# Later stores, first weights in two halves, and a refinement moved one stage on, in a fused state-space and feed-forward kernel

## The chip, the cores and the metric

The kernel runs on one core of a Trainium2 chip. The metric is the device time of one execution in microseconds; lower is better. A core has five engines that run their own instruction streams in order: TensorE (PE; its weight loads are shown as PEld), VectorE (DVE), ScalarE (ACT), GpSimdE (POOL) and SyncE (SP). DMA transfers are issued from the queues of SP, ACT and POOL.

## The reference

Two branches are computed from the layer-normalised input and added to the input itself. Sizes: L = 2048 positions, D = 576 channels, N = 128 states per channel, F = 4608 hidden units.

```
xn  = layernorm(x)                                   # per row of 576
dt  = exp(log_dt);  logdA = dt * (A_re + i A_im)
K[d, l] = Re sum_n C[d,n] * exp(logdA[d,n] * l) * dt[d] * B[d,n]     # l = 0..2047
y   = causal convolution over l of xn[:, d] with K[d, :]  (by FFT)  +  xn * Dskip
ffn = silu(xn @ w1) @ w2                              # (2048x576)(576x4608)(4608x576)
out = x + y + ffn
```

## The kernel before

**What is on TensorE.** Every float32 product is made from a high and a low part of each operand (three matmuls: high·high, high·low, low·high). ScalarE copies the high part (a cast), VectorE subtracts to get the low part. So each input block and each weight block needs a ScalarE copy and a VectorE subtraction before TensorE can use it: `put_xt` (L118) transposes a normalised block on TensorE into `pt`, makes `xh` (L123) and `xl` (L125); `split_w1` (L266) makes `w1h` (L274) and `w1l` (L276); `split_w2` (L286) does it for w2 (L292, L294); `up` (L298) makes the first product `ph` (L306 to L308), and from it `gf` (Silu, L314), `gh` (L315) and `gl` (L316); `down` (L318) makes the second product `po` (L336) and adds it to `acc` (L341).

**Stages.** The feed-forward part walks over two halves of the rows, nine chunks of hidden units and two blocks of 512 rows (the last chunks by a scheme of seven products for eight, `wino_ffn`). A second stream, `side()` (L1045), is woven into it step by step:

- `phase0` (L204): loads row blocks j in pairs, normalises them (`norm`, L179), turns them (`turned`, L222) and stores the normalised rows to the DRAM tensor `dxn` (L235), which only `spread` reads, much later. Blocks 8 to 15 also store their transposed form to `dxt` (L234) through one buffer `xt`, and are loaded back in the second half of the kernel.
- `natural` (L655): from A, B, C and log_dt the small tables f, rho, phi (128 states x 576 channels) and four real powers of the decay per channel, `ex`. It is a generator of several stages: after tanh (L705) comes a stage with the reciprocal root `r` (L709), its square (L710), three refinement operations on each of four column groups (L715 to L717), a store to `dexp` (L718) and the products of C and B up to L738; then a stage with Arctan (L742), a second reciprocal root (L744) and what follows.
- `kgen` (L772): 36 steps on VectorE and ScalarE that make tables S and C from f, rho, phi and pieces of `dexp` (`eb`, L802), multiplied on TensorE to `kp` (L883), `z` (L898), and stored to `d1k`. `spread` (L139) runs beside it.
- `spectral` (L919) and `tail` (L977): the convolution in the frequency domain and the way back.

**What sets the order.** The program is written in the order of the generators; a scheduler then places instructions on each engine's queue by its own estimate of times, so that neighbours can pass each other. Each engine executes its queue in order and waits on semaphores. `behind(ins)` keeps an instruction from being placed before `ins`. `tc.high_priority()` lets gf, gh, gl and the accumulations go ahead. `pins["gh"]` is the last `gh` written so far, `pins["sd"]` the last power of a variance on GpSimdE (L191).

**The first microseconds.** SP and ACT issue eight loads for row blocks 0 and 1, SP then six for the first two weight tiles `w1r` (`load_w1`, L245; each tile is 640 rows by 256 columns and is split in halves of 128), four for blocks 2 and 3, four for w2, eight for blocks 4 to 7. GpSimdE computes the powers of the variances and issues the `dxn` stores.

Of the kernel before, what the change touches and what calls it, by code (L numbers as in the profile page):

```python
# [10 lines left out]
F32 = mybir.dt.float32  # L11
F32R = mybir.dt.float32r
AF = mybir.ActivationFunctionType
ALU = mybir.AluOpType
# [3 lines left out]
P = 128  # L18
L = 2048
D = 576  # L20
# [21 lines left out]
def kernel(  # L42
# [21 lines left out]
    nc = tc.nc  # L64
# [18 lines left out]
    dxn = dram.tile([P, NJ, D], F32, name="dxn")  # L83
    dw2 = dram.tile([NFT - WINO_C * FT, P, 2, D], F32, name="dw2")
    dexp = dram.tile([P, 4 * D], F32, name="dexp")
# [26 lines left out]
    def new_xt(blk):  # L112
        xh = xtp.tile([P, NKT, 512], F32R, tag="xh", name=f"xh_{blk}")
        xl = xtp.tile([P, NKT, 512], F32R, tag="xl", name=f"xl_{blk}")
        x4 = xtp.tile([P, 512], F32R, tag="x4", name=f"x4_{blk}")
        return xh, xl, x4

    def put_xt(xh, xl, x4, src, low=None):  # L118

        pt = pss.tile([P, NKT, P], F32, tag="pss", name="pt")  # L120
        for kt in range(NKT):
            nc.tensor.transpose(pt[:, kt, :], src[:, kt * P:(kt + 1) * P], ident)
        nc.scalar.copy(xh, pt)  # L123
        with behind(low):
            nc.vector.tensor_sub(xl, pt, xh)  # L125
        pt = pss.tile([P, 512], F32, tag="pss", name="pt4")
        nc.tensor.transpose(pt[:64, :P], src[:, NKT * P:D], ident)
        pins["xt_s"] = nc.scalar.copy(x4[:64, :], pt[:64, :P]).ins
        pins["xt_v"] = nc.vector.tensor_sub(x4[64:, :], pt[:64, :P], x4[:64, :]).ins

    xts = {}
    pairs = {}
    pins = {}
    wino = {}

    def behind(ins):
        return tc.issue_after(ins) if ins is not None else nullcontext()
# [66 lines left out]
    def phase0(p0, js):  # L204
        j0 = js[0]
        if j0 < 8:
            xs = load_x(j0, accp, "acc", (nc.sync, nc.scalar) if j0 == 0 else (nc.sync,))
            acc.update(zip(js, xs))
            yield
        else:  # L210
            xs = load_x(j0, p0, "xj", (nc.sync,))
        if j0:
            with behind(pins["xt1"] if j0 == 2 else None):
                turned(p0, js, norm(p0, js, xs))
        else:
            xn = [norm(p0, (j,), (xj,)) for j, xj in zip(js, xs)]
            last = pins["xn"]
            for j in js:
                turned(p0, (j,), xn[j], None if j else last)
                pins[f"xt{j}s"] = pins["xt_s"]  # L220

    def turned(p0, js, xn, low=None):  # L222
        for i, j in enumerate(js):
            b, jj = divmod(j, 4)
            if b < 2:
                if jj == 0:
                    xts[b] = new_xt(b)
                c = slice(jj * P, (jj + 1) * P)
                xh, xl, x4 = xts[b]
                put_xt(xh[:, :, c], xl[:, :, c], x4[:, c], xn[:, i, :], low)  # L230
            else:
                xt = p0.tile([P, 9, P], F32R, tag="xt", name="xt", bufs=1)
                put_xt(xt[:, 0:4, :], xt[:, 4:8, :], xt[:, 8, :], xn[:, i, :])
                nc.gpsimd.dma_start(dxt[b - 2][:, :, jj * P:(jj + 1) * P], xt.bitcast(F32))  # L234
        nc.gpsimd.dma_start(dxn[:, js[0]:js[0] + len(js)], xn[:, :len(js)])  # L235

    def ffn():
        w2v = w2.rearrange("(t p) d -> p t d", p=P)
# [6 lines left out]
        def load_w1(half, c, t):  # L245

            f = c * FT + t
            first = half == 0 and c == 0
            r1 = (pa if first and t else w1x if t and w1x else wp).tile([P, 5, 2 * P], F32, tag="w1r", name="w1r", bufs=1)
            fs = slice(f * P, (f + 2) * P)  # L250
            eng = nc.sync
            eng.dma_start(r1[:, 0:4, :], w1[0:512, fs].rearrange("(k p) f -> p k f", p=P))
            eng.dma_start(r1[0:64, 4, :], w1[512:576, fs])
            pins["load"] = eng.dma_start(r1[64:128, 4, :], w1[512:576, fs]).ins
            R1[half, c, t] = r1

        def need_w1(half, c, t):
            if (half, c, t) not in R1:
                load_w1(half, c, t)

        def next_w1(half, c, t):
            new = (half, c + 1) if c + 1 < NCH else (half + 1, 0)
            if w1x and new < (1, WINO_C):
                load_w1(*new, t)
# [89 lines left out]
        for t in (0, 2):  # L354
            load_w1(0, 0, t)
# [17 lines left out]
        first, end = WINO_C * FT // 2, NFT // 2  # L373
# [39 lines left out]
        for i, blk in enumerate(plain[:-1]):  # L413
            half, c, b = blk
# [14 lines left out]
            for step in ("u0", "d0", "d1", "d2", "d3", "u1", "u2", "u3"):  # L429
                k = int(step[1])  # L430
# [224 lines left out]
    def natural(nat):  # L655
# [3 lines left out]
        v = nc.vector  # L659

        def tl(name):
            return nat.tile([NP, NT, NS], F32, tag=name, name=name)
# [34 lines left out]
        v.tensor_mul(aim, aim, dtb)  # L697
        lrT = nat.tile([P, D], F32, tag="lrT", name="lrT")
        turned(are, lrT)
        turned(aim, fT)  # L700

        ex = nat.tile([P, 4 * D], F32, tag="ex", name="ex")
        r = nat.tile([P, 4 * D], F32, tag="r", name="r")
# [3 lines left out]

        with behind(pins["gh"]):
            nc.scalar.activation(r, ex, AF.Abs_reciprocal_sqrt, bias=neg1)  # L709
        nc.scalar.activation(r, r, AF.Square)  # L710
        for i in range(0, 4 * D, D):

            c = slice(i, i + D)
            e = nat.tile([P, D], F32, tag="lrT", name="e")
            v.scalar_tensor_tensor(e, ex[:, c], 1.0, r[:, c], op0=ALU.subtract, op1=ALU.mult)  # L715
            v.scalar_tensor_tensor(r[:, c], e, 2.0, r[:, c], op0=ALU.add, op1=ALU.mult)
            v.scalar_tensor_tensor(ex[:, c], ex[:, c], 1.0, r[:, c], op0=ALU.add, op1=ALU.mult)  # L717
        nc.sync.dma_start(dexp, ex)  # L718
        pr, pi, t0, t1 = tl("pr"), tl("pi"), tl("t0"), tl("t1")
        v.tensor_mul(pr, cr, br)  # L720
        v.tensor_mul(t0, ci, bi)
# [16 lines left out]
        v.tensor_scalar(t1, t1, 1.0, None, op0=ALU.add)  # L738
        yield

        with behind(pins["gh"]), behind(pins["xo"]):
            last = nc.scalar.activation(t0, t0, AF.Arctan).ins  # L742
        with behind(last):
# [301 lines left out]
    def side():  # L1045
# [13 lines left out]
        with tc.tile_pool(name="kf", bufs=1) as kfp:  # L1059
            for n in ("f", "rho", "phi"):  # L1060
                kf[n] = kfp.tile([P, D], F32, name=n + "T")
            with tc.tile_pool(name="nat", bufs=1) as nat, tc.tile_pool(name="pb", bufs=2) as pb:
                nt = natural(nat)
                tiles = iter(range(8, NJ, 2))
                for at, tables in ((0.0, 1), (0.02, 0), (0.035, 0), (gate_of(1), 1), (0.06, 0), (gate_of(2), 1), (0.08, 0), (0.085, 1)):
                    yield at
                    if tables:
                        next(nt, None)
                    else:
                        j = next(tiles)  # L1070
                        with behind(pins["gl"]):
                            for _ in phase0(pb, (j, j + 1)):
                                pass
            with behind(pins["sd"]):
                nc.gpsimd.dma_start(f1, cf1)
            nc.sync.dma_start(vt, cv)
            with tc.tile_pool(name="up", bufs=1) as up, tc.tile_pool(name="w1x", bufs=1) as more:
                sp = spread(up)
                for n, at in enumerate(kgen()):
                    if n > 1:  # L1080
                        w1x = more
                        next(sp, None)
                    yield marks[0] + at * (marks[1] - marks[0])
                for _ in sp:
                    pass
# [16 lines left out]
    sd, fg = side(), ffn()  # L1102
# [85 lines left out]
```

## Time and profile before

| | |
|---|---|
| median of 3 runs | 1108.67 us (1108.48 to 1112.02) |
| profiled execution | 1109.05 us |
| its span, first to last instruction | 1107.2 us |
| granted TensorE clock, mean | 0.999 |
| busy, TensorE / VectorE / ScalarE / GpSimdE | 1089.8 / 949.5 / 722.3 / 141.1 us |
| moved by DMA | 173.67 MB |

The profile shows one execution. "Busy" counts the time in which an engine has at least one instruction running. In a timeline row the first number is the start in us, the second the duration; then engine, source line, operation, output tile <- input tiles, shapes, the number of merged instructions, and in brackets the idle time of that engine just before and what released it. A row of waits gives the total, the number of times and the longest.

### The profile page before, as it was taken

How to read it: one execution, taken by the hardware profiler on the slowest of the kernel's cores; microseconds unless marked ns; L12 is line 12 of the kernel's file. 1: busy time of each engine (PE TensorE's matmuls, PEld its weight loads, DVE VectorE, ACT ScalarE, POOL GpSimd, SP SyncE). 2: the span in 40 equal slices, each digit the busy share in tenths (PEclk: the TensorE clock that was granted, in tenths of full speed). 3: DMA queues.
4: the chain of work that ended last, by engine and by line, in shares of the span. 5: the costliest groups of instructions: out<-in, count | busy, mean ns of one | idle time of the engine just before them, and what ended most of it. 6: DMA issues, size and time to landing. Idle time of an engine off the chain costs nothing.

```text
span 1107.2 us, 23071 instructions
## 1 busy us (share of the span) xinstructions
PE 1089.8 (98%) x9101; PEld 986.7 (89%) x9101; DVE 949.5 (86%) x1615; ACT 722.3 (65%) x1284; POOL 141.1 (13%) x246
## 2 busy tenths in 40 slices
PE   6999999999999999999999999999999999999998
PEld 5988989898998888898999899899999999999787
DVE  6699989999999999999999997988988888886323
ACT  4475456676777676766767656877777787775320
POOL 1112100000000000000330002111111211111220
PEclk9999999999999999999999999999999999999999
DMA  8536552355253534447974246455555655554984
GB/s 255 162 109 217 167 166 89 115 145 153 94 161 110 144 132 119 166 110 260 236 197 93 81 88 193 146 173 177 150 163 177 181 167 155 178 161 107 242 222 112
DMA packets 162412, 173.67 MB, mean 157 GB/s; under 512 B 88560, under 2 KB 128128, under 8 KB 161664
## 3 DMA queue, kind: packets, MB, share of 16 engines
q1 hardware_dynamic: 137360, 105.35, 34.5%
q0 software_dynamic: 24272, 65.38, 19.4%
q10 hardware_dynamic: 672, 1.48, 0.5%
q8 instruction: 72, 1.18, 0.4%
q14 instruction: 36, 0.29, 0.1%
HBM read 109.64 MB, written 62.60 MB: 156 GB/s over the span
## 4 chain that ended last, share of the span: by engine, by line
PE 85%; DVE 5%; DMA 4%; ACT 3%; issue 1%; SPq 0%; POOL 0%; ACTq 0%; DVEq 0%
PE po L336 38%; PE ph L306 18%; PE pb L463 6%; PE pc L463 3%; PE kp L883 3%; PE pk L1017 2%; PE pu L1017 2%; PE pb L1017 2%; PE pa L463 2%; PE z L898 1%; PE ph L308 1%; PE ph L307 1%; DMA acc<-in_A_u_dram 1%; DMA kl<-d1k 1%; PE pc L469 1%; PE pu L155 1%
## 5 line engine op out<-in xcount | busy, mean ns | idle before, releaser
L336 PE MATMUL po<-w,gh 128*128 128x288 f32 x2304 | 474.2, 296 | 0.9 <-DVE acc L341 0.9
L336 PEld LDWEIGHTS po<-w,gh 128*128 128x128 f32 x2304 | 375.2, 188 | 16.7 <-issue 3.3
L336 PE MATMUL po<-w,gl 128*128 128x288 f32 x1152 | 333.6, 295 | 0.0
L336 PEld LDWEIGHTS po<-w,gl 128*128 128x128 f32 x1152 | 214.9, 188 | 1.7
L341 DVE TENSOR_TENSOR acc<-po,acc 128x288 f32<-128x288 f32 x296 | 129.7, 450 | 54.6 <-PE po L336 53.2
L306 PE MATMUL ph<-xh,w1h 128*128 128x512 f32 (+1 forms) x368 | 99.7, 388 | 1.7 <-ACT gf L314 1.3
L306 PE MATMUL ph<-xh,w1l 128*128 128x512 f32 (+1 forms) x368 | 98.3, 384 | 0.0
L306 PE MATMUL ph<-xl,w1h 128*128 128x512 f32 (+1 forms) x368 | 98.2, 384 | 0.0
L314 ACT ACTIVATE gf<-ph 128x512 f32<-128x512 f32 (+1 forms) x92 | 53.0, 578 | 51.4 <-PE ph L308 32.4
L306 PEld LDWEIGHTS ph<-xl,w1h 128*128 128x128 f32 x368 | 68.0, 191 | 13.4
L306 PEld LDWEIGHTS ph<-xh,w1l 128*128 128x128 f32 x368 | 66.7, 190 | 12.2 <-DVE w1l L276 0.2
L306 PEld LDWEIGHTS ph<-xh,w1h 128*128 128x128 f32 x368 | 65.0, 191 | 12.0 <-ACT gf L314 1.9
L840 ACT ACTIVATE c<-th,magic 128x1040 f32<-128x1040 f32 x36 | 42.0, 1167 | 41.5 <-DVE C L861 27.4
L158 POOL DMA_DIRECT2D d1u<-u x32 | 17.5, 547 | 393.9 <-ACT u L157 392.5
L842 ACT ACTIVATE c<-th 128x1040 f32<-128x1040 f32 x36 | 38.7, 1075 | 41.0 <-DVE th L841 41.0
L316 DVE TENSOR_TENSOR gl<-gf,gh 128x512 fp32r<-128x512 f32 (+1 forms) x92 | 60.2, 657 | 4.0 <-ACT gh L315 3.7
L922 POOL DMA_DIRECT2D m<-in_cm_dram x64 | 33.9, 531 | 215.8 <-PE pu L1017 135.9
L315 ACT CAST gh<-gf 128x512 fp32r<-128x512 f32 (+1 forms) x92 | 55.2, 603 | 8.9 <-PE po L336 7.9
L480 DVE TENSOR_TENSOR gl<-gf,gh 128x512 fp32r<-128x512 f32 x56 | 37.8, 688 | 23.1 <-ACT gh L479 22.7
L860 DVE TENSOR_TENSOR S<-th,C 128x1024 f32<-128x1024 f32 x36 | 43.9, 1218 | 7.4 <-ACT th L843 7.3
L841 DVE SCALAR_TENSOR_TENSOR th<-c,th 128x1040 f32<-128x1040 f32 x36 | 44.3, 1231 | 0.3 <-ACT c L840 0.3
L824 DVE TENSOR_TENSOR th<-vt,fT 128x1040 f32<-128x1040 f32 x36 | 44.2, 1231 | 0.2
(269 smaller groups left out, 2370.9 us busy)
## 6 DMA issues: line engine op xcount, KB each, us to landing
w1r<-in_B_w_dram SPq DMA_DIRECT2D x36, 512.0 KB, 4.1
dw<-w SPq DMA_DIRECT2D x28, 576.0 KB, 4.7
w<-dw POOLq DMA_DIRECT2D x28, 576.0 KB, 5.8
w2r<-in_B_w_dram SPq DMA_DIRECT2D x44, 288.0 KB, 4.7
d1u<-u POOLq DMA_DIRECT2D x32, 288.0 KB, 2.8
d1k<-stage SPq DMA_DIRECT2D x18, 512.0 KB, 6.4
ul<-d1u SPq DMA_DIRECT2D x32, 288.0 KB, 2.9
kl<-d1k SPq DMA_DIRECT2D x32, 288.0 KB, 3.6
```

The lines of the kernel that those rows point to most:

```text
L306: nc.tensor.matmul(ph, w[:, kt, :], v[:, kt, a:e], start=n + kt == 0, stop=False)
L314: nc.scalar.activation(gf, ph, AF.Silu)
L315: pins["gh"] = nc.scalar.copy(gh, gf).ins
L316: pins["gl"] = nc.vector.tensor_sub(gl, gf, gh).ins
L336: pins["pe"] = nc.tensor.matmul(po[:, :HD], gs[g][:, js], ws[:, w, hs], start=n == 0 and j not in begun, stop=n == 3 * len(terms) - 1, ski ...
L341: nc.vector.tensor_add(acc[j][:, hs], po[:, :HD], acc[j][:, hs])
L463: pins["pe"] = nc.tensor.matmul(dst, a[:, kt], v[:, kt], start=start and n == 0, stop=stop and n == 5, skip_group_check=True).ins
L824: nc.vector.tensor_mul(split(th), row(vt[:, 0:65], 65), col(fT, i, 65))
L840: nc.scalar.activation(c65, th, AF.Identity, bias=magic)
L841: nc.vector.scalar_tensor_tensor(th, c65, MAGIC, th, op0=ALU.subtract, op1=ALU.subtract)
L860: nc.vector.tensor_mul(ov3, t[:, :, 0:64].rearrange("n d (x y) -> n d x y", y=32), mv3)
L1017: nc.tensor.matmul(dst, st, mv[:, hs], start=n == 0, stop=n == 3 * len(terms) - 1)
```

## The change

Three edits:

1. `turned` no longer issues the store to `dxn` directly: it appends it to a list `held`, and from the second pair of blocks on all held stores are issued, each behind the last power of a variance. So the stores of blocks 0 and 1 come after the power for blocks 2 and 3, together with the store of that pair.
2. The first weight tile is loaded in two column halves of 128, the first from ScalarE's queue, the second from SP's; three DMAs become six.
3. In `natural` the square of `r`, the twelve refinement operations and the store to `dexp` leave the stage after tanh and stand at the beginning of the next stage, the square behind the last `gh` at that point, ahead of the Arctan.

```diff
@@ tile_ssm_ffn_kernel
+    held = []
@@ turned
-        nc.gpsimd.dma_start(dxn[:, js[0]:js[0] + len(js)], xn[:, :len(js)])
+        held.append((dxn[:, js[0]:js[0] + len(js)], xn[:, :len(js)]))
+        while js[0] > 1 and held:
+            with behind(pins["sd"]):
+                nc.gpsimd.dma_start(*held.pop(0))
@@ load_w1
-            fs = slice(f * P, (f + 2) * P)
-            eng = nc.sync
-            eng.dma_start(r1[:, 0:4, :], w1[0:512, fs].rearrange("(k p) f -> p k f", p=P))
-            eng.dma_start(r1[0:64, 4, :], w1[512:576, fs])
-            pins["load"] = eng.dma_start(r1[64:128, 4, :], w1[512:576, fs]).ins
+            for eng, a, e in ((nc.scalar, 0, P), (nc.sync, P, 2 * P)) if first and t == 0 else ((nc.sync, 0, 2 * P),):
+                fs = slice(f * P + a, f * P + e)
+                eng.dma_start(r1[:, 0:4, a:e], w1[0:512, fs].rearrange("(k p) f -> p k f", p=P))
+                eng.dma_start(r1[0:64, 4, a:e], w1[512:576, fs])
+                pins["load"] = eng.dma_start(r1[64:128, 4, a:e], w1[512:576, fs]).ins
@@ natural, stage after tanh
         with behind(pins["gh"]):
             nc.scalar.activation(r, ex, AF.Abs_reciprocal_sqrt, bias=neg1)
-        nc.scalar.activation(r, r, AF.Square)
-        for i in range(0, 4 * D, D):
-            c = slice(i, i + D)
-            e = nat.tile([P, D], F32, tag="lrT", name="e")
-            v.scalar_tensor_tensor(e, ex[:, c], 1.0, r[:, c], op0=ALU.subtract, op1=ALU.mult)
-            v.scalar_tensor_tensor(r[:, c], e, 2.0, r[:, c], op0=ALU.add, op1=ALU.mult)
-            v.scalar_tensor_tensor(ex[:, c], ex[:, c], 1.0, r[:, c], op0=ALU.add, op1=ALU.mult)
-        nc.sync.dma_start(dexp, ex)
@@ natural, next stage
         yield
+        with behind(pins["gh"]):
+            nc.scalar.activation(r, r, AF.Square)
+        for i in range(0, 4 * D, D):
...
+        nc.sync.dma_start(dexp, ex)
         with behind(pins["gh"]), behind(pins["xo"]):
             last = nc.scalar.activation(t0, t0, AF.Arctan).ins
```

More of the change, by code (lines that the diff above doesn't have):

```diff
@@ L739, in natural @@
         yield
+        with behind(pins["gh"]):
+            nc.scalar.activation(r, r, AF.Square)
+        for i in range(0, 4 * D, D):
+            c = slice(i, i + D)
+            e = nat.tile([P, D], F32, tag="lrT", name="e")
+            v.scalar_tensor_tensor(e, ex[:, c], 1.0, r[:, c], op0=ALU.subtract, op1=ALU.mult)
+            v.scalar_tensor_tensor(r[:, c], e, 2.0, r[:, c], op0=ALU.add, op1=ALU.mult)
+            v.scalar_tensor_tensor(ex[:, c], ex[:, c], 1.0, r[:, c], op0=ALU.add, op1=ALU.mult)
+        nc.sync.dma_start(dexp, ex)
         with behind(pins["gh"]), behind(pins["xo"]):
```

## The prediction

> **What bounds the kernel now.** I read the page first, then what TensorE waits for, then the busy time by stretch, then the timeline around each edit.
>
> ```profile
> PE 1089.8 (98%) x9101; PEld 986.7 (89%) x9101; DVE 949.5 (86%) x1615; ACT 722.3 (65%) x1284; POOL 141.1 (13%) x246
> ...
> PE 85%; DVE 5%; DMA 4%; ACT 3%; issue 1%; SPq 0%; POOL 0%; ACTq 0%; DVEq 0%
> ```
>
> TensorE is busy for 98% of the 1107.2 us span and makes 85% of the chain that ended last. The change adds no matmul and takes none away, so it can win only idle time of TensorE: 1107.2 − 1089.8 = 17.4 us in all. The waits (us in total, times, longest) and the busy time by stretch say where that lies:
>
> ```profile
> PE pt L122 <- DVE xn L195: 7.9, 3, 6.9
> PE ph L306 <- ACT gf L314: 1.3, 3, 0.9
> ...
> 0.00:30.00 30.00, 20.32 (x128) 18.09 (x129) 19.58 (x52) 14.20 (x31) 4.64 (x11) 1.00 0.90 254
> 100.00:148.00 48.00, 48.00 (x304) 43.92 (x303) 39.04 (x72) 27.27 (x45) 8.57 (x10) 1.00 0.66 215
> 150.00:645.00 495.00, 493.93 (x5055) 444.84 (x5054) 481.93 (x712) 339.34 (x505) 37.34 (x72) 1.00 0.49 140
> 1060.00:1107.00 47.00, 42.40 (x403) 36.67 (x402) 13.77 (x29) 5.90 (x12) 3.12 (x4) 0.97 0.60 145
> ```
>
> (Columns: length; busy us of PE, PEld, DVE, ACT, POOL; granted clock; DMA share; GB/s.) 9.7 us of the idle time is in the first 30 us, 4.6 in the last 47, which the change does not touch. From 150 to 645 TensorE loses 1.1 us in 495, but VectorE is 97% busy there: a second engine almost at its bound, close behind.
>
> **Part 1: the held stores.** In the first microseconds the profile shows:
>
> ```profile
> 7.04 0.15 DVE L190 TENSOR_SCALAR sd<-mv 128x1 f32<-128x1 f32 x1
> 7.20 0.61 POOL L235 DMA_DIRECT2D dxn<-xn  x1 [1.16 <-DVE sd L190]
> 7.84 0.58 POOL L191 TENSOR_TENSOR sd<-sd,mhalf 128x1 f32<-128x1 f32 x1
> 8.10 0.58 ACT L123 CAST xh<-pt 128x512 fp32r<-128x512 f32 x1 [5.40 <-PE pt L122]
> 8.46 0.58 DVE L195 TENSOR_SCALAR xn<-acc,mv,sd 128x576 f32<-128x576 f32 x1 [1.26 <-POOL sd L191]
> 10.24 0.58 ACT L123 CAST xh<-pt 128x512 fp32r<-128x512 f32 x1 [0.78 <-PE pt L122]
> 10.88 1.23 PE L306 MATMUL ph<-xh,w1h 128*128 128x256 f32 x4 [0.46 <-ACT xh L123]
> ```
>
> The variance of the second row block is ready at 7.19 (7.04 + 0.15). GpSimdE takes its power only at 7.84, because the issue of the first block's store (0.61 us) stands before it. In the changed order both powers precede all stores, so the power starts near 7.24 and what follows in a chain, xn, its transpose, the copy xh and the first ph matmul, comes 0.6 us earlier: 10.88 → 10.28.
>
> The second gain is that 2 × 288 KB leave a busy moment:
>
> ```profile
> w1r<-in_B_w_dram SPq DMA_DIRECT2D x36, 512.0 KB, 4.1
> d1k<-stage SPq DMA_DIRECT2D x18, 512.0 KB, 6.4
> dxn<-xn POOLq DMA_DIRECT2D x2, 288.0 KB, 6.8
> ```
>
> At the 254 GB/s of the first 30 us they take 590 / 254 = 2.3 us of transfer. Behind them land the rows of block pair (2, 3), which the statistics at 15.15 await:
>
> ```profile
> 15.15 1.54 DVE L186 BATCH_NORM_STATS2 st<-acc 128x6 f32<-128x288 f32 x4 [1.70 <-DMA acc<-in_A_u_dram]
> 16.61 1.54 DVE L276 TENSOR_TENSOR w1l<-w1r,w1h 128x640 fp32r<-128x640 f32 x2
> 20.29 0.66 PE L122 MATMUL pt<-ident,xn 128*128 128x128 f32 x4 [0.16 <-DVE xn L195]
> 21.42 0.57 ACT L123 CAST xh<-pt 128x512 fp32r<-128x512 f32 x1
> 22.98 1.22 PE L306 MATMUL ph<-xh,w1h 128*128 128x256 f32 x8
> ```
>
> In the changed order all four w1l go ahead of these statistics, so they would start near 14.6 even though the data may be there by 13. From their start to pt it is now 5.14 us; less the w1l pair (1.54), which no longer lies between, 3.6: xn is ready at 18.2. TensorE, 0.6 us earlier and without waiting for w1l, gets there at about 19.4, so pt does not wait. From pt to the next ph it is now 2.69 us (22.98 − 20.29); of that some 0.4 is ScalarE reaching xh late, since at 21.42 it had been busy with the other normalised row. I take 2.3: ph at 21.7 instead of 22.98, **−1.3 us**. Bounds: 0.3 (stalls stay and only part of the start survives) to 2.1 (TensorE warmed up and waiting only for xn at 18.2: 18.2 + 2.7 = 20.9). The three stores then run after the power of pair (2, 3), when the next loads, for rows 4 to 7, are under way; nothing waits for dxn before the spread stage, and I cost this at 0, at most those 2.3 us, of which VectorE's queue hides the most.
>
> **Part 2: the halved first weights.** They change no byte count. ScalarE has 5.40 us of idle time before 8.10, so three issues on its queue (0.4 to 0.6 us each, like those on SP) hide there; its first copy needs only its own half. Twice as many packets of half the size have no row. The nearest are w1r as it is (512 KB in 4.1 us) and the d1k store of much smaller packets (512 KB in 6.4): from 0 to +2.3 us for the tile, nearer to w1r since the pieces are only halved. I take +0.3, hidden by the 2.3 us that the held stores free. Below zero is possible as well, since two queues issue at once; nothing on the path waits for it.
>
> **Part 3: the square and the refinement.** Here TensorE waits now:
>
> ```profile
> 75.04 2.13 ACT L710 ACTIVATE r<-r 128x2304 f32<-128x2304 f32 x1
> 77.19 1.28 ACT L314 ACT_TABLE_LOAD   x1
> 78.48 0.60 ACT L314 ACTIVATE gf<-ph 128x512 f32<-128x512 f32 x1
> ...
> 77.98 0.29 PE L336 MATMUL po<-w,gl 128*128 128x288 f32 x1
> 79.13 1.18 PE L306 MATMUL ph<-xh,w1h 128*128 128x512 f32 x4 [0.86 <-ACT gf L314]
> ```
>
> Without the square the table load and gf come 2.1 us earlier. But the changed order also puts this ph ahead of the twelve po matmuls that stand before it now (12 × 0.133 = 1.6 us), so TensorE arrives 1.6 earlier: the wait falls from 0.86 to about 0.4. **−0.45 us**, between 0 and −0.86.
>
> Where they go:
>
> ```profile
> 79.81 0.75 DVE L715 SCALAR_TENSOR_TENSOR e<-ex,r 128x576 f32<-128x576 f32 x1
> 102.06 0.75 DVE L717 SCALAR_TENSOR_TENSOR ex<-ex,r 128x576 f32<-128x576 f32 x1
> ...
> 101.47 0.88 ACT L200 ACTIVATE xj<-xj,mb,sd 128x576 f32<-128x576 f32 x1
> 107.97 0.60 ACT L314 ACTIVATE gf<-ph 128x512 f32<-128x512 f32 x1
> ```
>
> The first and last of twelve refinement operations: 12 × 0.74 = 8.9 us of VectorE, now between 80 and 103; in the changed order they follow the square, which stands after a later gh, near 98. VectorE is idle for 48 − 39.04 = 9.0 us between 100 and 148, which holds them. The square (2.13) goes before the arctangent group: from 101.47 to the end of gf it is 7.1 us now, in the changed order with two transposed copies and a scaling inside (1.7) and the square 10.9. TensorE has 28 + 36 po and 28 ph between the two ph it concerns, 64 × 0.133 + 28 × 0.228 = 14.9, so some 2 to 4 us cover it: 0. If that cover were gone, up to 2.13. The dexp store moves with it in SP's queue, ahead of one w1r load whose buffer is not yet free; nobody reads dexp before the tables begin.
>
> **Part 4: what the new order does to the table stage.**
>
> ```profile
> 246.34 4.65 PE po L336 x35
> 251.88 2.75 PE ph L306 x12
> ...
> 148.22 0.06 DVE L792 MEMSET magic<- 128x1 f32 x1 [3.26 <-DMA dxt<-xt]
> ...
> 205.06 0.68 DVE L861 SCALAR_TENSOR_TENSOR C<-c,C 128x512 f32<-128x512 f32 x1
> 208.90 0.34 PE L883 MATMUL kp<-C 128*32 128x64 f32 x8
> ```
>
> (The first two rows give 0.133 and 0.229 us for a matmul.) The tables of the second pair are complete at 205.74, and kp starts at 208.90: 3.2 us to spare. In the changed order TensorE has 22 po and 16 ph fewer before this kp, 6.6 us; VectorE has one accumulation, two gl and two w2 fewer before those tables, about 3.1. So 3.2 − 6.6 + 3.1 = −0.3: **+0.3 us**, between 0 and +2. The later groups stand within 4 us of where they were, and after 650 the order is the same.
>
> Sum: −1.3 − 0.45 + 0.3 = −1.45. The profiled execution took 1109.05 (span 1107.2), 0.4 above the median of 1108.67; from the median, 1108.67 − 1.4 = **1107.3**.
>
> **Rivals.** *The clock decides the start* (0.12).
>
> ```profile
> 11.91 1.05 PE L306 MATMUL ph<-xl,w1h 128*128 128x256 f32 x4
> 18.77 0.64 PE L306 MATMUL ph<-xl,w1h 128*128 128x256 f32 x4
> ```
>
> Four equal matmuls take 1.05 us early and 0.64 later, with a granted clock of 1.00 written beside both. If the fast spacing begins at the same instant as now, 0.6 us won at the slow spacing are worth only 0.3 later: 1107.6. The Trainium skill (TensorE: Matmul & The Clock Gate, What's actually happening) says that the array starts at half rate and that the window that releases it runs freely, not from the kernel's start; the trace agrees on the two spacings, and whether the instant moves no run here shows.
>
> *The head gives nothing* (0.18): the first weights, on two queues and in smaller packets, or the loads of pair (2, 3) become the late ones. For it: VectorE waits 1.70 us for such a load. Against: 2.3 us of traffic leave. Then −0.45 + 0.3: 1108.5.
>
> *The tables come late, and the kernel gets slower* (0.17). VectorE begins the tables at 148.22 once the last dxt store has landed; eight such stores follow each other through one xt buffer, each behind a subtraction in VectorE's queue, where nine more microseconds now stand. If the tables begin at the same time while TensorE runs 1.75 us earlier, it waits 0.3 + 1.75 at the second kp and is 0.3 behind now; every further microsecond is lost in full, as VectorE cannot catch up at 97%. It decides from a start 3 us later than now (about 151); at 4 us it is 4.3 slower, 1113.0. Against it: the idle 9.0 us, and transposes of later blocks that stand 8 us earlier in the order.
>
> *All bounds fall well* (0.13): head −2.1, the wait at 79 gone (−0.86), about 1 of the 1.1 us from 150 to 645 gone: −4.0, 1104.7.
>
> **Numbers.** The forecast has 0.40, with 1106.0 to 1108.7 of its own. A measurement of this kernel can tell about 0.3%, 3.3 us (under 1105.3 or over 1112.0). Faster: 0.13. Slower: 0.17. Within: 0.40 + 0.12 + 0.18 = 0.70. The range takes all of the last and the near part of both others: 1105.2 to 1111.9.
>
> **What would show it.** Right: the second power directly behind the first at about 7.2, the first ph at 10.3, the ph after pt at 21.7, a wait of 0.4 near 77 and one under 1 us at the second kp. Wrong: a first ph that is not earlier; ScalarE's first weight copy waiting for a transfer; a wait for gf after the arctangent; tables that begin after 151 and waits of TensorE at several kp.

## The result, and the profile after

The changed kernel takes **1114.56 us** (median of 6 runs, 1113.31 to 1116.07) against 1108.83 before (6 runs, 1108.48 to 1112.02): ratio 1.0052, 95% interval 1.0042 to 1.0061. It is slower by 5.7 us; the forecast was 1107.3 with a range to 1111.9. The profiled execution took 1115.41 (span 1113.6), 0.85 over its median, so the trace shows a loss of 6.4.

The page's busy line of the changed kernel (its source lines are 4 or 5 higher than before: L310 was L306, L345 was L341):

```profile
PE 1091.7 (98%) x9101; PEld 987.2 (89%) x9101; DVE 950.3 (85%) x1615; ACT 723.1 (65%) x1284; POOL 141.2 (13%) x246
```

What its TensorE waits for beside the start (us in total, times, longest):

```profile
PE po L340 <- DVE acc L345: 4.1, 4, 1.7
PE ph L310 <- ACT gf L318: 1.5, 4, 0.5
PE pa L467 <- ACT pa L531: 1.4, 1, 1.4
PE pt L127 <- DVE xt L125: 1.1, 1, 1.1
```

And its busy time by stretch, columns as in the prediction:

```profile
0.00:30.00 30.00, 20.87 (x141) 19.20 (x142) 21.06 (x58) 15.15 (x34) 5.06 (x12) 1.00 0.90 262
80.00:100.00 20.00, 20.00 (x125) 18.14 (x124) 13.64 (x30) 13.47 (x20) 3.17 (x4) 1.00 0.72 214
100.00:148.00 48.00, 45.61 (x278) 40.57 (x276) 41.42 (x73) 21.46 (x38) 8.27 (x9) 1.00 0.54 177
150.00:645.00 495.00, 492.56 (x5041) 443.09 (x5042) 478.00 (x705) 339.11 (x505) 37.40 (x72) 1.00 0.50 142
```

TensorE is busier in the first 30 us (20.87 against 20.32), and from 100 to 148, where it had no idle time at all, it loses 2.4 us; from 150 to 645 it loses 2.4 where it lost 1.1. VectorE has moved 6 us of work out of 80 to 100 (13.64; the same stretch before had 19.63):

```profile
80.00:100.00 20.00, 20.00 (x118) 17.66 (x117) 19.63 (x38) 7.98 (x15) 3.72 (x4) 1.00 0.62 184
```

A busy TensorE is not one at its speed. So I also took, from each trace, the time from the start of one matmul to the start of the next, less the median that before has for matmuls of the first one's shape, and summed it by stretch. This is lost time of TensorE in us, waits and slow matmuls together, of one execution each:

| kernel | 0–30 | 30–90 | 90–157 | 157–645 | 645–1028 | rest | sum |
|---|---|---|---|---|---|---|---|
| before | 8.1 | 1.4 | 0.3 | 16.3 | 3.3 | 9.9 | 39.3 |
| changed | 6.1 | 0.9 | 6.7 | 18.2 | 3.7 | 9.9 | 45.6 |

The whole loss is there (differences taken before rounding): −1.9 at the head, −0.5 up to 90, **+6.5 between 90 and 157**, +1.9 behind it up to 645, +0.4 up to 1028.

**First place, 95 to 106 us.** The timeline of the changed kernel: VectorE's rows, then ScalarE's, then TensorE's.

```profile
95.72 0.76 DVE L742 SCALAR_TENSOR_TENSOR e<-ex,r 128x576 f32<-128x576 f32 x1 [0.52 <-ACT r L737]
...
96.76 0.75 DVE L743 SCALAR_TENSOR_TENSOR r<-e,r 128x576 f32<-128x576 f32 x1
100.79 0.95 DVE L752 TENSOR_TENSOR are<-t,bi 96x768 f32<-96x768 f32 x1 [3.29 <-ACT bi L749]
101.67 0.45 DVE L187 BATCH_NORM_STATS2 st<-xj 128x6 f32<-128x288 f32 x1
...
104.45 0.67 DVE L125 TENSOR_TENSOR xt<-pt,xt 128x512 fp32r<-128x512 f32 x1
...
98.62 1.28 ACT L749 ACT_TABLE_LOAD   x1
99.91 0.85 ACT L749 ACTIVATE bi<-t 96x768 f32<-96x768 f32 x1
...
105.27 0.27 PE L127 MATMUL pt<-ident,xj 128*64 128x128 f32 x1 [1.07 <-DVE xt L125]
```

The product of L752 comes behind the second refinement operation and waits 3.29 us for ScalarE's tables and roots. Behind it in VectorE's queue stand the other ten refinement operations, which could run, and xt, for which TensorE then waits (1.1 us idle, 1.2 by the sums above). Before, the refinement ran there.

**Second place, 141 to 155 us.** The timeline of the changed kernel: VectorE, ScalarE, TensorE.

```profile
145.15 0.06 DVE L797 MEMSET magic<- 128x1 f32 x1 [3.00 <-DMA dxt<-xt]
...
145.33 2.37 DVE L829 TENSOR_TENSOR th<-vt,fT 128x1040 f32<-128x1040 f32 x2
147.62 0.68 DVE L320 TENSOR_TENSOR gl<-gf,gh 128x512 fp32r<-128x512 f32 x1
148.22 0.45 DVE L345 TENSOR_TENSOR acc<-po,acc 128x288 f32<-128x288 f32 x1
...
149.11 0.44 ACT L815 COPY pw<-eb 128x128 f32<-128x128 f32 x1 [3.12 <-DMA eb<-dexp]
149.33 0.64 ACT L318 ACTIVATE gf<-ph 128x512 f32<-128x512 f32 x1
...
144.49 1.07 PE L310 MATMUL ph<-xh,w1l 128*128 128x512 f32 x4
...
148.72 0.53 PE L340 MATMUL po<-w,gh 128*128 128x288 f32 x2 [1.66 <-DVE acc L345]
...
150.02 1.29 PE L310 MATMUL ph<-xh,w1h 128*128 128x512 f32 x4 [0.51 <-ACT gf L318]
151.11 1.91 PE L310 MATMUL ph<-xl,w1h 128*128 128x512 f32 x4
```

The same place in stretches of 1 us (the last three columns are the granted clock, the DMA share and GB/s):

```profile
147.00:148.00 1.00, 0.07 (x1) 0.00 (x0) 1.00 (x2) 0.00 (x0) 0.00 (x0) 1.00 0.40 100
148.00:149.00 1.00, 0.28 (x2) 0.28 (x3) 1.00 (x3) 0.00 (x0) 0.00 (x0) 1.00 0.28 70
149.00:150.00 1.00, 0.51 (x4) 0.28 (x3) 1.00 (x3) 0.86 (x2) 0.00 (x0) 1.00 0.00 0
150.00:151.00 1.00, 0.98 (x4) 0.85 (x5) 1.00 (x2) 1.00 (x2) 0.00 (x0) 0.98 0.01 3
151.00:152.00 1.00, 1.00 (x4) 0.70 (x4) 0.97 (x3) 1.00 (x2) 0.00 (x0) 0.50 0.97 348
```

Two queues are blocked here. On VectorE an accumulation and a gl stand behind the tables' first instruction, which waits for the last dxt store, and behind two products (2.37 us). On ScalarE a gf stands behind a copy that waits for `eb`, a piece of dexp that SP begins to load at 145.29, once the last dxt store has landed (145.04); the dexp store itself had landed at 131.52. TensorE waits for the accumulation and then for that gf, which ends last: the ph of 150.02 starts when it is done. By these rows an earlier accumulation alone would have won nothing, and an earlier gf alone some 0.5 us.

Then the granted clock is 0.50, and four matmuls take 1.91 us instead of 1.07. By the sums above TensorE loses 1.8 + 0.7 us in the two waits and 1.5 at half speed (eight ph matmuls take 154.47 − 151.11 us instead of 8 x 0.228). With the 1.2 of the first place, and 0.6 at 129 where TensorE waits for a gf, this is 5.8 of the 6.5. Before, the same VectorE instruction waited 3.26 us and cost nothing, since the gl stood ahead of it in the queue, and on ScalarE the gf (147.31) ahead of the copy (155.72).

### The profile page after: what moved, and what is told of

The parts are those of the page before. It is cut to its first block, busy times and chain, and to the rows that moved or that the text cites. A ratio compares the mean times of both kernels' runs of the same rounds, so it can differ in the third digit from the quotient of the medians.

```text
span 1113.6 us, 23081 instructions
## 1 busy us (share of the span) xinstructions
PE 1091.7 (98%) x9101; PEld 987.2 (89%) x9101; DVE 950.3 (85%) x1615; ACT 723.1 (65%) x1284; POOL 141.2 (13%) x246
## 3 DMA queue, kind: packets, MB, share of 16 engines
q0 software_dynamic: 24272, 65.38, 19.3%
## 4 chain that ended last, share of the span: by engine, by line
PE 85%; DMA 4%; DVE 4%; issue 3%; ACT 2%; POOL 0%; SPq 0%; ACTq 0%; DVEq 0%; POOLq 0%
PE po L340 37%; PE ph L310 17%; PE pb L467 6%; PE pc L467 3%; PE kp L888 3%; PE pb L1022 2%; PE pk L1022 2%; PE pu L1022 2%; PE z L903 2%; PE pa L467 2%; PE ph L311 1%; PE ph L312 1%; PE pc L473 1%; PE pu L156 1%; PE pu L157 1%
## 5 line engine op out<-in xcount | busy, mean ns | idle before, releaser
L340 PEld LDWEIGHTS po<-w,gh 128*128 128x128 f32 x2304 | 375.4, 188 | 19.8 <-DVE acc L345 5.2
L345 DVE TENSOR_TENSOR acc<-po,acc 128x288 f32<-128x288 f32 x296 | 129.3, 451 | 54.9 <-PE po L340 53.2
L310 PE MATMUL ph<-xh,w1h 128*128 128x512 f32 (+1 forms) x368 | 100.2, 390 | 2.0 <-ACT gf L318 1.5
L310 PE MATMUL ph<-xl,w1h 128*128 128x512 f32 (+1 forms) x368 | 100.2, 388 | 0.0
L310 PE MATMUL ph<-xh,w1l 128*128 128x512 f32 (+1 forms) x368 | 99.2, 385 | 0.0
L310 PEld LDWEIGHTS ph<-xl,w1h 128*128 128x128 f32 x368 | 68.0, 192 | 12.7
L310 PEld LDWEIGHTS ph<-xh,w1l 128*128 128x128 f32 x368 | 67.1, 190 | 12.0
L310 PEld LDWEIGHTS ph<-xh,w1h 128*128 128x128 f32 x368 | 65.0, 191 | 13.6 <-ACT gf L318 3.0
```

The lines of the kernel that those rows point to most:

```text
L310: nc.tensor.matmul(ph, w[:, kt, :], v[:, kt, a:e], start=n + kt == 0, stop=False)
L340: pins["pe"] = nc.tensor.matmul(po[:, :HD], gs[g][:, js], ws[:, w, hs], start=n == 0 and j not in begun, stop=n == 3 * len(terms) - 1, ski ...
L345: nc.vector.tensor_add(acc[j][:, hs], po[:, :HD], acc[j][:, hs])
```

## The experiments

The 95% intervals are those of the ratio to before, in runs on the same chip. "Held and halves" is the kernel before with the first two edits only.

**Each edit alone.** The diffs are the parts of the change.

> The kernel before with the held stores alone. Theory M (the moved square and refinement alone make the loss, the head edits gain): the second power directly behind the first, the ph after pt earlier by 0.3 to 1.3 us, no new wait of TensorE between 100 and 155 us; 1107.5 to 1108.5. Rival O (every edit shifts the list scheduler's order, and any new order costs some us somewhere): 1110 or more, with new waits far behind the head. Rival J (the loss needs the earlier head and the moved refinement together): as M here.

> The kernel before with the halved first weights alone. M: within 0.7 us of before, 1108 to 1109.5; the first ph at 10.6 to 11.2 us. O: 1110 or more, with waits far behind the head. J: as M here.

> The kernel before with the square and the refinement moved alone, the head as before. M: the waits of TensorE for xt near 107, for VectorE's accumulation near 150 and the half-rate ph matmuls behind it are here as in the changed kernel, without the head's gain of 1.6: 1115 to 1117. O: a part of the loss only, 1110 to 1112, since each edit has its share. J: without the head's lead of TensorE the wait near 150 is under 0.5 us and the loss 0 to 2: 1108 to 1111.

> The changed kernel with the square and the refinement back in their old place: held stores and halved weights alone. M: the head's gain without the loss, 1107.0 to 1107.6 (before less 1.2 to 1.8). O: 1110 or more. J: as M here, 1107.0 to 1107.6.

| kernel | median us | ratio | interval |
|---|---|---|---|
| held stores alone | 1108.68 | 0.9994 | 0.9984 to 1.0003 |
| halved weights alone | 1108.20 | 0.9994 | 0.9985 to 1.0003 |
| moved refinement alone | 1115.73 | 1.0062 | 1.0048 to 1.0075 |
| held and halves | 1107.83 | 0.9991 | 0.9982 to 1.0000 |

The third edit makes the loss by itself, without the first two: J and O fall, and M stands for the loss, though the head gains less than its 1.2 to 1.8. With the third edit alone TensorE waits at the same places as in the changed kernel; at the tables the gf is now the long wait (2.0) and the accumulation the short one (0.35):

```profile
PE ph L306 <- ACT gf L314: 2.7, 3, 2.0
PE po L336 <- DVE acc L341: 2.6, 4, 1.7
PE pt L127 <- DVE xt L125: 1.1, 1, 1.1
```

Held and halves gain about 1 us of the 2.0 that the head shows in their trace (lost time 6.0 against 8.1). The 2.0 is not the edits' alone, since the moved refinement alone, whose head has neither of them, loses only 6.4 there (more on this under part 1 below). And a part goes to a wait for a weight copy, which before's trace does not have. TensorE's timeline of held and halves:

```profile
126.99 1.20 PE L310 MATMUL ph<-xh,w1h 128*128 128x512 f32 x4 [0.88 <-ACT w1h L278]
```

**Square or refinement?** One kernel puts only the square back, one adds twelve unused operations to VectorE at the new place, one adds an unused square to ScalarE there.

```diff
 # square_home: the changed kernel
             nc.scalar.activation(r, ex, AF.Abs_reciprocal_sqrt, bias=neg1)
+        nc.scalar.activation(r, r, AF.Square)
...
-        with behind(pins["gh"]):
-            nc.scalar.activation(r, r, AF.Square)
 # refine_twice: held and halves, ahead of the Arctan
+        with behind(pins["gh"]):
+            for i in range(12):
+                e = nat.tile([P, D], F32, tag="lrT", name="e")
+                v.scalar_tensor_tensor(e, ex[:, i % 4 * D:(i % 4 + 1) * D], 1.0, r[:, i % 4 * D:(i % 4 + 1) * D],
+                                       op0=ALU.subtract, op1=ALU.mult)
 # square_twice: held and halves, ahead of the Arctan
+        with behind(pins["gh"]):
+            nc.scalar.activation(r, r, AF.Square)
```

> The changed kernel with the square alone put back behind the reciprocal roots; the twelve refinement operations keep their new place in the text. Theory Q (the refinement's place in VectorE's queue is set by when the square is done, not by the text; the late square pushes it behind the arctangent's tables): the refinement goes back to 78 to 103 us, no wait of TensorE at 105 and 149, 1107.3 to 1108.3 as with held and halved loads alone. Rival P (the place in the text decides): 1113 to 1115, as the changed kernel.

> Held stores and halved weights, square and refinement in their old place, and twelve more operations of the refinement's first kind on VectorE (8.9 us, their results unused) at the place to which the change moves it. Theory F (8.9 us more of VectorE between 100 and 148 do not fit into its idle 9.0 us, since it stands in order behind others): TensorE waits near 149 and loses 3 us or more, 1110.5 to 1114. Rival R (not the load but the order: the accumulations behind the tables' first instructions): VectorE takes them in its gaps, under 1 us, 1107.5 to 1109.

> Held stores and halved weights, square and refinement in their old place, and a second square (2.1 us on ScalarE, its result unused) at the new place ahead of the arctangent. Theory A (ScalarE's longer chain, square, table, arctangent, table, roots, makes TensorE wait for gf and for the transposed copies): +1 to +2.1 us, 1109 to 1110. Rivals Q and F: TensorE's queue covers it, under 0.5 us, 1107.5 to 1108.3.

Square home: 1108.43, 0.9996 (0.9987 to 1.0004). The text still has the refinement a stage later, but with r ready VectorE takes it at the old place, and nothing is lost, as theory Q expected. Square twice: 1108.63, 0.9997 (0.9988 to 1.0005): 2.1 us more of ScalarE ahead of the Arctan cost nothing by themselves, as the prediction had it; A falls. Refine twice: 1110.45, 1.0015 (1.0006 to 1.0023), that is 2.7 us over held and halves by the ratios: at the lower end of F, but without F's wait near 149. VectorE took most of it in between 100 and 148 (before: 39.04 us busy):

```profile
100.00:148.00 48.00, 47.70 (x301) 43.43 (x300) 45.81 (x81) 25.62 (x42) 7.87 (x9) 1.00 0.59 191
```

45.81 of 48 us are busy, TensorE lost 0.3 us here; the price came later (18.9 of lost time from 157 to 645, against 16.3).

**The order at the tables.**

```diff
 # the changed kernel; the tables are begun at a later step, and their first instructions held
-                for at, tables in (..., (0.08, 0), (0.085, 1)):
+                for at, tables in (..., (0.08, 0), (0.085, 1), (0.125, 1)):
...
-            nc.vector.memset(magic, MAGIC)
+            with behind(pins["gl"]):
+                nc.vector.memset(magic, MAGIC)
 # the same for the other set and the first product th
```

> The changed kernel with the tables' first VectorE instructions (the two sets and the first two products) held behind the second of the gl that now follow them, so that an accumulation and two gl no longer stand behind the wait for the last dxt store. Theory R (that order makes the wait of 1.8 us at 149 and the cold clock behind it, 1.4 us): both go, 2.5 to 3.5 us won against the changed kernel, 1111 to 1112. Rival F (VectorE is too full by then, and the wait moves elsewhere): under 1 us won, 1113.5 to 1114.6.

1111.28, 1.0022 (1.0014 to 1.0031): 3.3 us won against the changed kernel by the ratios, as theory R expected. The same instruction now finds the stores landed, TensorE does not wait there, and the clock stays at 1.00. But ScalarE's order is another one too: a gf now stands ahead of the copy for `eb`. The edit frees both queues, and these runs do not tell what each is worth. VectorE's and ScalarE's timeline of this kernel:

```profile
143.69 0.68 DVE L320 TENSOR_TENSOR gl<-gf,gh 128x512 fp32r<-128x512 f32 x1
144.32 0.06 DVE L798 MEMSET magic<- 128x1 f32 x1
...
145.22 0.59 ACT L318 ACTIVATE gf<-ph 128x512 f32<-128x512 f32 x1
147.99 0.47 ACT L817 COPY pw<-eb 128x128 f32<-128x128 f32 x1 [2.18 <-DMA eb<-dexp]
```

The stretch in which the changed kernel's TensorE stood still:

```profile
147.00:148.00 1.00, 1.00 (x10) 1.00 (x9) 0.97 (x2) 0.01 (x1) 0.00 (x0) 1.00 1.02 359
```

**The gap at 97 us.** First the product of L752 alone is held behind xt of block 11; then a kernel without the refinement; and an attempt at something better.

```diff
 # xt_first: the changed kernel, with pins["xv11"] the low part of block 11
-        v.tensor_mul(rc, t1, bi)
+        with behind(pins["xv11"]):
+            v.tensor_mul(rc, t1, bi)
 # square_on_gpsimd: held and halves
-        nc.scalar.activation(r, r, AF.Square)
+        nc.gpsimd.tensor_tensor(r, r, r, op=ALU.mult)
```

> The changed kernel with one instruction held: VectorE's first product behind the second table's roots (line 752 of the changed kernel) goes behind the transposed copy of row block 11, not ahead of it. Theory X (the head-of-line block: VectorE stands 3.3 us for ScalarE's chain with the statistics and xt queued behind it, and what is late after it gives the bad order at 149): the waits at 105 and 149 and the half-rate matmuls go, 3.5 to 5 us won, 1109.5 to 1111. Rival F (the refinement's 8.9 us in 100 to 148 cost it, wherever the product stands): under 1.5 us won, 1113 or more.

> The changed kernel without the twelve refinement operations (the unrefined values go to the tables; 8.9 us of VectorE left out); the square stays late, and the product of line 752 still stands ahead of the transposed copy. Theory X: the wait near 105 stays (1 us or more), VectorE catches up behind it, the wait at 149 shrinks; 1108.5 to 1111. Rival F: no wait at 149, 1106.5 to 1108.

> A version that might beat both: held stores and halved weights, refinement in its old place, the square as a multiplication on GpSimdE instead of ScalarE. ScalarE loses its 2.1 us ahead of the table load, so the wait of 0.8 us for gf near 77 goes, and the refinement starts one GpSimdE operation after the roots, at 78 to 80 us, no later than now; against held and halved loads alone 0.3 to 0.9 us won, 1107 to 1107.8. Rival: GpSimdE's operation takes 4 us or more, the refinement slides behind the arctangent's tables as in the changed kernel, and it is 1 to 4 us slower.

`xt_first`: 1112.51, 1.0035 (1.0023 to 1.0047): some 1.9 us won (the intervals overlap a little), less than X said, and the wait for xt is still there, even longer (1.6). The next instruction in the queue took over the block: statistics that wait for a load. VectorE's timeline of `xt_first`:

```profile
101.77 0.82 DVE L187 BATCH_NORM_STATS2 st<-xj 128x6 f32<-128x288 f32 x2 [3.44 <-DMA xj<-in_A_u_dram]
...
104.57 0.67 DVE L125 TENSOR_TENSOR xt<-pt,xt 128x512 fp32r<-128x512 f32 x1
```

What went is the second place: with the products later, VectorE's queue has the gl ahead of the tables again, and ScalarE's the gf ahead of the copy. `drop_refine`: 1110.72, 1.0020 (1.0012 to 1.0029): without the refinement's 8.9 us at all it is still slower than before, with the wait for xt at 1.5; F falls in its simple form. (Its trace is of an execution of 1108.27 us, the fastest of twelve and 2.5 under their median.) `square_on_gpsimd`: 1112.35, 1.0031 (1.0019 to 1.0043). GpSimdE needs 4.0 us for what ScalarE did in 2.1 (its timeline),

```profile
70.43 4.02 POOL L714 TENSOR_TENSOR r<-r 128x2304 f32<-128x2304 f32 x1 [3.30 <-ACT r L713]
```

but the refinement was not late for that (its first step came at 79.10). A new order brought new waits, the largest of 1.6 us for a copy of w2 near 148. Both the expectation and its rival's mechanism were wrong.

**Gap and tables, the four combinations.** Now both instructions that wait, the product and the statistics of blocks 14 and 15, are held behind xt of block 11, without and with the tables held.

```diff
 # norm, added to xt_first
-                nc.vector.bn_stats(out=st[:, i, h, :], in_=xs[i][:, h * HD:(h + 1) * HD])
+                with behind(pins["xv11"] if js[0] == 14 else None):
+                    nc.vector.bn_stats(out=st[:, i, h, :], in_=xs[i][:, h * HD:(h + 1) * HD])
```

> The changed kernel with both instructions that stand between the first refinement steps and the transposed copy of block 11 on VectorE (the product of line 752, which waits for ScalarE's chain, and the statistics of blocks 14 and 15, which wait for a load) held behind that copy, so that refinement steps fill the gap at 97 to 101 us; the order at the tables is as in the changed kernel. Theory C (two places: the gap costs the wait at 105, the tables' order the wait at 149 and the cold clock): the wait at 105 goes, the one at 149 stays; 1 to 1.5 us won, 1113 to 1114. Theory X (the gap is the source of all): 3.5 us or more won, under 1111. Rival F: under 0.5 won.

> The same with the tables' first VectorE instructions held behind the second of the following gl as well. Theory C: both waits go, 4 to 5 us won against the changed kernel, 1109.6 to 1110.6; what is left against held and halved loads alone (1.5 to 2.5) is the 8.9 us of VectorE added between 100 and 148, as with the twelve unused operations. Rival F: no better than with the tables held alone, 1111.3.

| ratio to before (interval) | tables as changed | tables behind gl |
|---|---|---|
| gap as changed | 1.0052 (1.0042 to 1.0061) | 1.0022 (1.0014 to 1.0031) |
| gap filled | 1.0041 (1.0029 to 1.0054) | 1.0022 (1.0013 to 1.0032) |

The wait for xt falls to 0.6 in both kernels with the gap filled. Alone that wins about 1.2 us (the intervals overlap), with the tables held nothing more: C holds for the tables, not for the sum. X falls.

**Nothing at the old place.** Held and halves, refinement left out, square early.

> Held stores and halved weights, square in its old place, the twelve refinement operations left out altogether (the unrefined values go to the tables): VectorE does 8.9 us less between 78 and 103 and nothing more later. Theory G (the old place was a filling: without it VectorE stands idle there behind an instruction that waits, and the transposed copy behind it is late): a wait near 105 of 0.7 us or more, no gain in all, 1108 to 1110.5. Rival F (only the load of VectorE after 100 us counts, and here it is no greater): no wait near 105, 1106 to 1107.8.

1111.79, 1.0024 (1.0015 to 1.0033): slower than before with 8.9 us *less* for VectorE. There is no wait for xt, so G's mechanism is not it, and F is as wrong. VectorE is idle at 98 to 101, waiting for bi, and the tables begin at 139.49; TensorE's waits stand further on (one of 1.4 for an accumulation, one of 1.1 for a copy of w2), in an order that shares little with before's.

The lost time of TensorE for all of these, by the same sums as above:

| kernel | 90–157 | 157–645 |
|---|---|---|
| before; held; halves; held and halves; square home; square twice | 0.2 to 1.8 | 16.1 to 16.6 |
| refine twice | 0.8 | 18.9 |
| moved refinement alone | 6.8 | 18.0 |
| tables behind gl | 1.6 | 19.3 |
| xt first | 3.5 | 19.3 |
| gap filled; with tables | 4.2; 1.8 | 18.2; 19.4 |
| drop refine | 2.7 | 16.9 |
| refine gone early | 1.0 | 19.8 |
| square on GpSimdE | 3.1 | 19.7 |

The first line holds the kernels in which VectorE's order around the tables is that of before. All others lose 0.3 to 3.7 us more than these between 157 and 645, whether VectorE has more to do, the same, or less; the 0.3 comes from that one execution of 1108.27 us without the refinement.

No version clearly beats before. Held and halves is the nearest, 0.9991 with an interval that ends at 1.0000.

## Why the prediction was wrong, point by point

**The failed step is part 3, "Where they go".** It put the twelve operations into VectorE's 9.0 idle us between 100 and 148 and the square under 2 to 4 us of TensorE's work, and wrote 0 for both. The moved refinement alone measures +6.9 us (1.0062 of 1108.9). The square's 0 was right as an amount of work (square twice: none). The refinement's 0 was not: the same 8.9 us added at the new place cost 2.7 us though VectorE took most of them in. And the largest piece is no amount of work at all but an order: with the refinement at the new place the tables' first instruction stands ahead of a gl and an accumulation on VectorE, and the copy for `eb` ahead of a gf on ScalarE, and their waits (3.00 and 3.12 us) stop TensorE. The prediction had quoted the first of them from before (3.26 us). Beginning the tables later, behind that gl, gives back 3.3 of the 5.7 us. The prediction summed idle time, and did not ask of each waiting instruction who would stand behind it in the new queue. It had done so for the order around the arctangent, not for the start of the tables. It had also counted idle time of TensorE alone; 1.5 us of the loss are matmuls at half speed.

**"If the cover is gone".** The refinement was itself a cover: at 97 us it filled the time in which VectorE waits for ScalarE's tables and for a load. Moved, it stands behind that wait. The gap cost 1.1 us of waiting for xt; filling it won about 1.2, and nothing once the tables were held.

**Part 1, the head.** The sum was about right, the steps were not, and that the sum fits the trace is in part luck. The second power starts at 7.61, directly behind its variance, but 0.23 us earlier instead of 0.6, since the statistics of block 1 waited 0.57 for their load. The first weight copy then waits for its half. Rows of the changed kernel's timeline, GpSimdE, ScalarE, TensorE:

```profile
7.61 0.56 POOL L192 TENSOR_TENSOR sd<-sd,mhalf 128x1 f32<-128x1 f32 x1 [1.60 <-DVE sd L191]
9.47 0.72 ACT L278 CAST w1h<-w1r 128x640 fp32r<-128x640 f32 x1 [0.30 <-DMA w1r<-in_B_w_dram]
10.74 1.23 PE L310 MATMUL ph<-xh,w1h 128*128 128x256 f32 x4 [0.52 <-ACT xh L123]
...
14.32 0.69 PE L310 MATMUL ph<-xh,w1l 128*128 128x256 f32 x4
...
19.18 0.60 PE L122 MATMUL pt<-ident,xn 128*128 128x128 f32 x4
...
21.40 1.22 PE L310 MATMUL ph<-xh,w1h 128*128 128x256 f32 x8
```

The first ph came at 10.74, not 10.28; the ph after pt at 21.40 (forecast 21.7), 1.58 earlier than before, since pt no longer waits and the fast spacing of the matmuls begins at 14.32. But the moved refinement alone, without either head edit, comes to the same ph at the same time, although its first ph is as late as before's. Its TensorE timeline:

```profile
10.96 1.22 PE L306 MATMUL ph<-xh,w1h 128*128 128x256 f32 x4 [0.46 <-ACT xh L123]
...
14.32 0.64 PE L306 MATMUL ph<-xh,w1l 128*128 128x256 f32 x4
...
21.41 1.22 PE L306 MATMUL ph<-xh,w1h 128*128 128x256 f32 x8
```

Its fast spacing begins at 14.0, that of before at 15.5. Over all the traces this instant lies between 13.4 and 16.6 us, so one trace each cannot say what the head edits are worth. The runs can: held and halves together win 1.0 us (0 to 2.0), forecast 1.3, and their trace spends 0.9 on a new wait at 127.

**The wait for gf.** Forecast 0.4 near 77; it is 0.34, and 0.5 us are won (forecast 0.45):

```profile
75.36 1.19 PE L310 MATMUL ph<-xh,w1h 128*128 128x512 f32 x4 [0.34 <-ACT gf L318]
```

**The second kp** (+0.3) does not wait: it starts at 206.33, its tables are complete at 204.72. The loss from 157 to 645 was 1.9 there, at other places, the longest an accumulation for which TensorE waits 1.7 at 357.

**The rivals.** "The tables come late" had the sign and nearly the size (1113.0), but its condition was not met: the tables begin at 145.15, 3 us *earlier* than before, and the second kp does not wait. What it missed is that they begin ahead of the feed-forward's own instructions. Its chance of 0.17 was low for a change that alters the order of three engines for 550 us, in a stretch where VectorE is 97% busy. "The clock decides the start" had as its condition that the instant of the fast spacing stays. Over the traces it moves by 3 us, and not with the first matmul: that starts at 6.95 in before, with the fast spacing from 15.5, and at 7.99 in held and halves, with the fast spacing from 15.0. "The head gives nothing" is not excluded by an interval that ends at 0.

**What stays open.** With both places held, 2.4 us over before remain, about 3.4 over held and halves. They lie between 157 and 645. Every kernel with another order shows something like it, even one in which VectorE does less (refinement left out, square early). In five of the kernels with the moved refinement (the changed one, the moved refinement alone, tables behind gl, and both with the gap filled) TensorE waits 0.4 to 0.9 us for an accumulation near 220, and 1.7 for one between 353 and 358, where before has 0.9 at 350; in the others the waits lie elsewhere. Whether before's order is simply a good one among many, or one cause runs through all, these runs do not tell.

## What to carry to other kernels

Before moving work into an engine's idle time, list in the new queues, of every engine, each instruction that waits and read what stands behind it: an in-order engine's idle microseconds are not a store into which work can be poured, and a wait that costs nothing today costs its length when a feeder of the bound engine slips behind it. Ask also what the moved work was covering at the place that it leaves. Where a scheduler orders the queues, test a small edit against a neutral reordering: here every kernel with another order around the tables was 1.7 to 6.9 us slower than before, more than the head edits were worth.

## What the runs showed of the hardware

TensorE fell to half clock without being idle for long. In the changed kernel the trace's record of the granted clock has half clock from 150.96 to 154.38 us, 3.413 us, and full clock ahead of it from 14.43, 136.53 us or 40 times as long. In before the full clock lasts 1088.85 us, 319 times as long, and in every other trace a whole number of times as well. So in these traces the clock changes on a grid of 3.413 us. Two stretches of this grid in the changed kernel, then one of the kernel with the gap filled and one of the kernel with the tables behind gl:

```profile
147.55:150.96 3.41, 1.73 (x8) 1.37 (x9) 3.41 (x7) 1.82 (x4) 0.00 (x0) 1.00 0.10 25
150.96:154.38 3.42, 3.42 (x10) 2.64 (x9) 3.36 (x6) 1.83 (x3) 0.00 (x0) 0.50 0.98 312
...
147.20:150.61 3.41, 1.81 (x8) 1.43 (x9) 3.38 (x7) 1.89 (x4) 0.00 (x0) 1.00 0.07 18
...
352.91:356.33 3.42, 1.72 (x13) 1.49 (x12) 3.39 (x7) 2.98 (x5) 0.00 (x0) 1.00 0.22 86
```

In the stretch whose end brought the fall TensorE was busy for 1.73 us. With the gap filled it had waits of about the same sum at the same place (1.06 + 1.45 us), was busy for 1.81, and kept its clock; with the tables behind gl it kept it after a stretch with 1.72. So about half a stretch of work can go either way, and busy time, whose ends are modelled, does not tell which.

The Trainium skill (TensorE: Matmul & The Clock Gate, What's actually happening) has a free-running window of some 3.4 us and half rate after an idle one. The trace agrees on the length of 3.4 us; that the window must be idle does not fit, since the one ahead of the fall holds 1.73 us of work. Waits of some 2.5 us in the middle of a kernel can so cost 1.5 us more, or nothing more; at what amount of work the clock falls, no run here shows.
